# Attention and a feed-forward layer on one core: batch 1's attention divided by queries

## The chip, the core and the metric

The kernel runs on one core of a Trainium2 chip. Its engines have a queue each and run in the order of their own queue: TensorE (PE) multiplies matrices from SBUF into PSUM, VectorE (DVE) and ScalarE (ACT) work on SBUF and PSUM, GpSimd (POOL) on SBUF, and SyncE (SP) issues DMAs. An instruction waits for others by semaphores, and everything behind it in the same queue waits with it. The metric is the device time of one execution in microseconds (us), less is better.

## The reference

Eight batches of eight heads with 576 tokens of 64 channels. Each head adds two attentions: a pooled one, over means of four neighbouring tokens, and a local one, where a token sees only those less than four away. The sum, 4608 tokens of 512 channels, goes through two matrices with g = h cos(h) between them. Everything is float32.

```python
out_d = sm_attn(q_d, k_d, v_d)            # means of 4 tokens: 144 x 144 per head
out_up = np.repeat(out_d, factor, axis=2)
mask = np.abs(pos[:, None] - pos[None, :]) < factor
...
out_local = np.matmul(attn, v)
x = (out_up + out_local)                  # to 4608 x 512
h = x @ w_in                              # 512 x 2048
g = h * np.cos(h)
return g @ w_out                          # 2048 x 512
```

## The kernel before

**Tiles and steps.** The 4608 tokens are cut into 12 tiles of 384 (`TT`), and the 2048 hidden channels into 16 chunks. A step is one tile with one chunk: `gemm1` (L741, 12 matmuls: the product is made of three, of high and low parts), an elementwise chain that makes g and splits it (L752 ACT, L753 DVE, L750 and L751 ACT with Sin and Square, L756 DVE, L758 or L759 the high part `gh`, L399 the low part `gl`), and, two steps later, `gemm2` (L777, 9 matmuls into PSUM banks). `PASSES` orders the steps: the first three tiles take four chunks each in turn (steps 0 to 3 tile 0, 4 to 7 tile 1, 8 to 11 tile 2, then the next four chunks, and so on to step 47), since the weights come in by and by. From step 48 on each tile takes all 16 chunks.

**Attention.** A unit is one batch and one pair of heads (four pairs a batch): `u_qk` and `u_v` load and pool, `u_s` makes scores and softmax (on PE L546 local and L555 pooled scores; on DVE L569 adds the mask, L574 and L582 take maxima, L399 subtracts, L610 to L614 sum and invert, L616 scales; on ACT L593 to L597 the Exp), `u_t` transposes (L634 on DVE, L650 on PE, L465 copies), and `u_pv` multiplies by v (L667 pooled, L679 local), adds both (L698) and writes the high and low parts of x (L713, L399) into the tile's buffers `x0h`, `x0l` and so on. Batches 0 and 1 (`b < NEARLY`) take one form, batches 2 to 7 another (scores at L539, output at L686, over a buffer `ptb`). 576 tokens are one and a half tiles: batch 0 fills tile 0 and half of tile 1, batch 1 the other half of tile 1 (its first 192 queries) and tile 2 (the other 384), batch 2 begins tile 3.

**Weights.** Each chunk's two matrices come as 64-bit floats, are loaded to `wdi` and `wdo` (L410) and split into high and low parts `wi` and `wo` (`w_split`, L420 to L433 and L399) over a small staging buffer `xxh`. Until the last of them is split, that buffer holds the place of tile 3's x. Buffers of late chunks (`wxi`, `wxo`) hold the q, k, v and softmax of batch 0's and 1's pairs 1 to 3 until those are through.

**Order.** Nothing is looped on the chip: a planner (`Plan`) takes every operation with a time at which it is wanted (`at(time, function, batch, pair)`; the time counts steps), gives it to an engine by its own costs (some may go to one of two engines), and writes out each engine's queue. In batch 1 (L833 to L835) `u_s` of pair i is wanted at -0.9 + i, `u_t` at -0.1 + i, `u_pv` at 0.7 + i. Where the planner expects PE to idle in the first 300 us, it puts fillers (L900): products of the identity that nobody reads, which keep the clock of PE up. ACT loads a table when it goes from Exp to Sin or back.

**The mask** of batches 0 and 1 (L325 to L342) has `NSEG + 1` = 7 segments of 32 float32 columns. POOL makes all of them by `affine_select`, and two segments get an edge for the first and the last token.

Of the kernel before, what the change touches and what calls it, by code (L numbers as in the profile page):

```python
# [300 lines left out]
def attn_ffn_kernel(ctx: ExitStack, tc: tile.TileContext, qT, kT, vdn, vl, w_in, w_out, out):  # L301
# [208 lines left out]
    def u_s(b, pr):  # L510
# [57 lines left out]
        for h in range(2):  # L568
            using(banks[h], pl.op("DVE", _dve(NSEG * BS), lambda h=h: dve.tensor_tensor(  # L569
                out=sml.get()[:, NSEG * h:NSEG * (h + 1)], in0=banks[h].get()[:, LQ:LQ + NSEG * BS].rearrange("p (s n) -> p s n", n=BS),  # L570
                in1=mask[:, h:h + NSEG] if b < NEARLY else band, op=ALU.add), r=[loc[h]] + zeroed[:1], pw=[sml]))
# [16 lines left out]
        m, su2 = 4 * SD, pl.buf(None)
        bd = lambda t: t.unsqueeze(3).broadcast_to([HD, 2, 2, SD])
        if early:  # L590

            def exps():
                act.activation(mxd.get(), mxd.get(), AF.Copy, scale=1.0 / 128.0)  # L593
                act.activation(sml.get(), sml.get(), AF.Exp, scale=0.125)
# [8 lines left out]
        else:  # L603
            def exps():
                act.activation(sml.get(), sml.get(), AF.Exp, scale=0.125)
                return act.activation(smd.get(), smd.get(), AF.Exp, scale=1.0 / 128.0)
# [1 line left out]
        for sm, part, size in ((sml, sul, n), (smd, sud, m)):
            if not (early and sm is smd):
                pl.op("DVE", _dve(size), lambda sm=sm, part=part: dve.tensor_reduce(  # L610
                    out=part(), in_=sm.get(), axis=AX.X, op=ALU.add), r=[sm, su], pw=[su2])
# [3 lines left out]
        for sm, part, size, bc in ((sml, sul, n, bl), (smd, sud, m, bd)):  # L615
            f = lambda e, sm=sm, part=part, bc=bc: lambda: e.tensor_tensor(out=sm.get(), in0=sm.get(), in1=bc(part()), op=ALU.mult)  # L616
# [11 lines left out]
    def u_t(b, pr):  # L628
# [14 lines left out]
        for h in range(2):  # L643
            bk = bank(b, "t")

            def t_mm(h=h, bk=bk):
                for kh in range(2):
                    for qh in range(2):
                        o = kh * SD + qh * HD
                        pe.transpose(bk.get()[:HD, o:o + HD], smd.get()[:, h, qh, kh * HD:(kh + 1) * HD], ident[:HD, :HD])  # L650
# [325 lines left out]
```

## Time and profile before

| | us |
|---|---|
| median of 3 runs | 1002.34 (1000.7 to 1004.37) |
| the profiled execution | 1000.14 |
| its span, first to last instruction | 998.3 |
| mean granted clock of PE | 0.996 |

A row of a view by lines reads: line, engine, operation, output<-input by the program's names, shape, count; then the busy time in us and the mean of one in ns; then how long the engine idled ahead of them, and for whom. A row of a timeline begins with the start and the duration in us, and ends, in brackets, with the idle time ahead of it. A row of the table by stage gives the stage in us and its length, then the busy time of PE, PEld (weight loads), DVE, ACT and POOL, each with its count, then the clock granted to PE (1.00 is full), the share of the DMA engines in use and GB/s. A row of waits names who waited for whom, the sum in us, how often, and the longest.

### The profile page before, as it was taken

Reading aid. Unit: us, or ns where it says so; the run is one execution under the profiler, and the core shown is the slowest. Engines: PE = TensorE matmul, PEld = TensorE weight load, DVE = VectorE, ACT = ScalarE, POOL = GpSimd, SP = SyncE. Lnnn points to the kernel's source line nnn. Section 1 sums busy time; section 2 is a strip of 40 time slices with the busy share of each in tenths; the row PEclk is TensorE's granted clock in tenths of the full one; section 3 lists DMA queues with packets and bytes.
Section 4 is the critical chain, followed back from the end, with each engine's and each line's share of the span. In section 5 each row is a group of like instructions: output and inputs, shape, how many; then the busy total and the mean of one; then the engine's idle time right before and its main releaser. Section 6 shows DMA issues by size and latency. Waiting matters only on the chain.

```text
span 998.3 us, 23933 instructions
## 1 busy us (share of the span) xinstructions
PE 984.4 (99%) x9958; PEld 847.8 (85%) x9958; DVE 678.2 (68%) x1362; ACT 610.1 (61%) x1174; POOL 227.3 (23%) x280
## 2 busy tenths in 40 slices
PE   8998999999999999999999999999999999999998
PEld 5566898899888888989888888888898888899997
DVE  6899999985698677464758957565658865433433
ACT  4467687876667647555556746555646665555554
POOL 6795334621344012010002202100002200000000
PEclk9899999999999999999999999999999999999999
DMA  8876723342464222110213312201212310000000
GB/s 236 251 246 214 232 107 52 68 64 40 79 139 118 75 73 57 60 50 28 77 49 93 102 44 74 69 25 37 64 53 74 124 53 7 35 1 1 32 1 32
DMA packets 41051, 80.70 MB, mean 81 GB/s; under 512 B 4976, under 2 KB 16240, under 8 KB 40944
## 3 DMA queue, kind: packets, MB, share of 16 engines
q1 hardware_dynamic: 37056, 72.11, 23.1%
q0 software_dynamic: 3888, 7.08, 5.0%
q8 instruction: 78, 1.28, 0.5%
q14 instruction: 29, 0.24, 0.1%
HBM read 57.93 MB, written 16.52 MB: 75 GB/s over the span
## 4 chain that ended last, share of the span: by engine, by line
PE 86%; DVE 3%; DMA 1%; ACT 1%; issue 1%; POOL 1%; SPq 0%; ACTq 0%; DVEq 0%; POOLq 0%
PE bank L777 39%; PE bank L741 38%; PE bank L539 2%; PE bank L686 2%; PE bank L555 1%; PE bank L667 1%; PE bank L650 1%; DMA q<-qT 1%; SPq L641 0%; DVE su L610 0%; DVE smd L616 0%; DVE tr L756 0%; PE bank L900 0%; DMA ptb<-sml 0%; DVE tr L753 0%
## 5 line engine op out<-in xcount | busy, mean ns | idle before, releaser
L777 PE MATMUL bank<-wo,gh 128*128 128x512 f32 x1152 | 363.5, 396 | 0.0
L777 PEld LDWEIGHTS bank<-wo,gh 128*128 128x128 f32 x1152 | 210.0, 188 | 38.0 <-issue 3.3
L777 PE MATMUL bank<-wo,gl 128*128 128x512 f32 x576 | 227.6, 395 | 0.0
L752 ACT ACTIVATE tr<-bank,bmagic 128x384 f32<-128x384 f32 x192 | 110.9, 577 | 116.2 <-PE bank L741 112.3
L756 DVE SCALAR_TENSOR_TENSOR tr<-tr,bank 128x384 f32<-128x384 f32 x192 | 104.9, 546 | 107.9 <-ACT tr L751 107.1
L753 DVE SCALAR_TENSOR_TENSOR tr<-tr,bank 128x384 f32<-128x384 f32 x192 | 105.7, 550 | 82.0 <-ACT tr L752 80.3
L750 ACT ACTIVATE tr<-tr 128x384 f32<-128x384 f32 x192 | 100.7, 524 | 75.9 <-DVE tr L753 75.3
L758 ACT ACTIVATE gh<-tr 128x384 fp32r<-128x384 f32 x163 | 85.3, 523 | 88.6 <-DVE tr L756 86.9
L399 DVE TENSOR_TENSOR gl<-tr,gh 128x384 fp32r<-128x384 f32 x154 | 92.4, 600 | 63.5 <-ACT gh L758 60.6
L777 PEld LDWEIGHTS bank<-wo,gl 128*128 128x128 f32 x576 | 108.0, 188 | 23.4
L741 PE MATMUL bank<-x0h,wi 128*128 128x384 f32 x384 | 107.0, 339 | 0.0
L741 PE MATMUL bank<-x1h,wi 128*128 128x384 f32 x384 | 106.9, 339 | 0.0
L741 PE MATMUL bank<-x2h,wi 128*128 128x384 f32 x384 | 106.8, 339 | 0.0
L741 PE MATMUL bank<-x3h,wi 128*128 128x384 f32 x384 | 106.5, 338 | 0.0
L399 POOL TENSOR_TENSOR gl<-tr,gh 128x384 fp32r<-128x384 f32 x38 | 44.9, 1183 | 269.6 <-DVE gh L759 183.8
L751 ACT ACTIVATE tr<-tr 128x384 f32<-128x384 f32 x192 | 100.8, 525 | 6.1
L741 PEld LDWEIGHTS bank<-x0h,wi 128*128 128x128 f32 x384 | 70.2, 188 | 2.4 <-DVE mxl L574 0.2
L741 PEld LDWEIGHTS bank<-x1h,wi 128*128 128x128 f32 x384 | 70.2, 188 | 2.4 <-issue 0.4
L741 PEld LDWEIGHTS bank<-x2h,wi 128*128 128x128 f32 x384 | 70.2, 188 | 2.2 <-DVE xxh L425 0.2
L741 PEld LDWEIGHTS bank<-x3h,wi 128*128 128x128 f32 x384 | 70.2, 188 | 2.0
L741 PE MATMUL bank<-x3l,wi 128*128 128x384 f32 x192 | 64.6, 336 | 0.4 <-DVE x3l L399 0.4
L741 PE MATMUL bank<-x1l,wi 128*128 128x384 f32 x192 | 64.5, 336 | 0.0
(199 smaller groups left out, 1456.3 us busy)
## 6 DMA issues: line engine op xcount, KB each, us to landing
vl<-vl SPq DMA_DIRECT2D x26, 384.0 KB
out<-ob SPq DMA_DIRECT2D x36, 256.0 KB
wdi<-w_in SPq DMA_DIRECT2D x16, 512.0 KB
wdo<-w_out SPq DMA_DIRECT2D x16, 512.0 KB
q<-qT SPq DMA_DIRECT2D x26, 292.0 KB
k<-kT SPq DMA_DIRECT2D x26, 292.0 KB
vd<-vdn SPq DMA_DIRECT2D x26, 288.0 KB
out<-ob POOLq DMA_DIRECT2D x27, 256.0 KB, 5.0
```

Source lines behind the costliest of these rows:

```text
L399: f = lambda e: lambda: e.tensor_tensor(out=out(), in0=in0(), in1=in1(), op=ALU.subtract)
L539: pe.matmul(banks[h].get()[BS * g:BS * (g + 1), c:c + BS], q.get()[hs, o:o + BS], k.get()[hs, o:o + BS], start=True, stop=True)
L555: pe.matmul(banks[h].get()[:HD, i * SD:(i + 1) * SD], qkd.get()[hs, 0, i * HD:(i + 1) * HD], qkd.get()[hs, 1, :], start=True, stop=True)
L686: pe.matmul(banks[e].get()[64 * h:64 * h + 64, o:o + 2 * BQ], v4[r, NSEG * h + n, :], pt[r, :, NSEG * h + n, :BQ], start=True, stop=True)
L741: pe.matmul(ph.get()[:, :m], w[:, i, kc, :], x[:, kc, :], start=(n == 0), stop=(n == 3 * KC - 1))
L750: act.activation(tr.get(), tr.get(), AF.Sin, scale=PI)
L751: return act.activation(tr.get(), tr.get(), AF.Square)
L752: pl.op("ACT", _act(m, True, 1), lambda: act.activation(tr.get(), h(), AF.Identity, bias=bmagic), r=[ph], w=[tr])
L753: pl.op("DVE", _dve(m), lambda: dve.scalar_tensor_tensor(out=tr.get(), in0=tr.get(), scalar=MAGIC, in1=h(), op0=ALU.subtract, op1=ALU.subt ...
L756: pl.op("DVE", _dve(m), lambda: dve.scalar_tensor_tensor(out=tr.get(), in0=tr.get(), scalar=0.5, in1=h(), op0=ALU.subtract, op1=ALU.mult), ...
L758: pl.op("ACT", _act(m, False), lambda: act.activation(gh.get(), tr.get(), AF.Copy), r=[tr], w=[gh], alts=[("DVE", _dve(m / 2), lambda: dve ...
L777: pe.matmul(o, (gh, gh, gl)[k].get()[:, sl], wo.get()[:, (0, 1, 0)[k]], start=(c == c0 and k == 0), stop=(c == c1 - 1 and k == 2))
```

## The change

Batch 1's units are divided. `PART = ((0, 1), (1, 3))` counts thirds of the queries: part 0 is the first 192, part 1 the other 384. `part_s`, `part_t` and `part_pv` do for a part what `u_s`, `u_t` and `u_pv` did for the whole, with the same instructions on fewer queries: 4 or 8 of the 12 local segments, 48 or 96 of the 144 pooled queries (as partitions of one score matrix, where the whole had two of 72). Buffers are cut out of the pair's own by `piece`. All four pairs' part 0 are wanted from -0.9 on, all part 1 from 3.1 on. `smd` gets 128 partitions, so the other forms name the part of it that they use (`[:HD]`).

The mask becomes nine segments in bf16. POOL makes one, DVE copies it to the others; batch 0's second bank takes segments 3 to 8 in place of 1 to 6, and the parts take 0 to 3 and 1 to 8.

```diff
-    mask = const.tile([P, NSEG + 1, BS], F32, name="mask")
+    mask = const.tile([P, 9, BS], BF16, name="mask")
...
-        pool.memset(mask, 0.0)
+        pool.memset(mask[:, 1:2], 0.0)
         for i in range(4):
-            h = mask[i * BS:(i + 1) * BS]
+            h = mask[i * BS:(i + 1) * BS, 1:2]
...
+        dve.tensor_copy(mask[:, 0:1], mask[:, 1:2])
+        dve.tensor_copy(mask[:, 2:9], mask[:, 1:2].broadcast_to([P, 7, BS]))
...
+    PART = ((0, 1), (1, 3))
...
+    def part_s(b, pr, part):
...
+        a0, a1 = PART[part]
+        na, ns, M = a1 - a0, 4 * (a1 - a0), 48 * (a1 - a0)
...
+        def l_mm():
+            for n in range(4 * a0, 4 * a1):
+                for h in range(2):
+                    for e in range(2):
...
+        def d_mm():
+            for h in range(2):
+                hs = slice(64 * h, 64 * h + 64)
+                pe.matmul(banks[h].get()[:M, :SD], qkd.get()[hs, 0, 48 * a0:48 * a1], qkd.get()[hs, 1, :], start=True, stop=True)
...
+            in1=mask[:, a0:a0 + ns], op=ALU.add), r=[loc], w=[sml]))
...
+        def exps():
+            act.activation(mxd.get()[:M], mxd.get()[:M], AF.Copy, scale=1.0 / 128.0)
+            act.activation(sml.get(), sml.get(), AF.Exp, scale=0.125)
+            for h in range(2):
+                ins = act.activation(smd.get()[:, h], banks[h].get()[:M, :SD], AF.Exp, bias=mxd.get()[:M, h:h + 1], scale=1.0 / 128.0,
+                                     accum_out=sud()[:, h:h + 1])
...
+    def part_t(b, pr, part):
...
+    def part_pv(b, pr, part):
...
+        tt = tile_of(b * S + 192 * a0)
+        a, m = b * S + 192 * a0 - FROM[tt], 192 * na
...
+    def u_s(b, pr, part=None):
+        if part is not None:
+            return part_s(b, pr, part)
...
-                in1=mask[:, h:h + NSEG] if b < NEARLY else band, op=ALU.add), r=[loc[h]] + zeroed[:1], pw=[sml]))
+                in1=mask[:, 3 * h:3 * h + NSEG] if b < NEARLY else band, op=ALU.add), r=[loc[h]] + zeroed[:1], pw=[sml]))
...
-        for t, f in ((-4.0 + 0.5 * i, u_qk), (-2.4 + 0.5 * i, u_v), (-0.9 + i, u_s), (-0.1 + i, u_t), (0.7 + i, u_pv)):
+        for t, f in ((-4.0 + 0.5 * i, u_qk), (-2.4 + 0.5 * i, u_v)):
             at(t, f, 1, i)
+        for piece_, t0 in ((0, -0.9), (1, 3.1)):
+            for d, f in ((0.0, u_s), (0.8, u_t), (1.6, u_pv)):
+                at(t0 + i + d, f, 1, i, piece_)
```

The planner makes new queues out of this. On PE, before, the last pair of batch 1 stands directly ahead of tile 1's first GEMM (`x1h` with chunk 0's weights), between fillers (L900); L539 and L555 behind them are batch 2's first scores:

```order
L650 MATMUL bank<-ident,wxi_218 72x72 x8
...
L667 MATMUL bank<-wxo_275 64x144 x4
...
L900 MATMUL bank<-ident_b 128x512
L679 MATMUL bank<-wxi_564,wxo_587 64x24 x48
...
L539 MATMUL bank<-k,q 32x32 x48
L555 MATMUL bank<-qkd 72x144 x4
L741 MATMUL bank<-x1h,wi_947 128x384
```

Now, at the end of the same attention (L619 transposes, L649 local output and L638 pooled output of a part; L907 is `gemm1`, L943 `gemm2`, L1069 the filler):

```order
L638 MATMUL bank<-wxi_208 64x96 x4
L907 MATMUL bank<-x1h,wi_1443 128x384
...
L649 MATMUL bank<-wxo_398,wxi_551 64x24 x32
L943 MATMUL bank<-wo_1224,gh 128x512 x2
...
L619 MATMUL bank<-ident,wxi_220 72x96 x4
L649 MATMUL bank<-wxi_556,wxo_585 64x24 x32
L638 MATMUL bank<-wxo_277 64x96 x4
L1069 MATMUL bank<-ident_b 128x512
...
L701 MATMUL bank<-k,q 32x32 x48
L717 MATMUL bank<-qkd 72x144 x4
...
L907 MATMUL bank<-x2h,wi_911 128x384
```

All four GEMM steps of tile 1 have moved between the parts of the attention, and what follows the last pair is tile 2's first GEMM. In all, PE has 82 fillers ahead of step 0 and 84 from there to tile 1's first GEMM before; now 80 ahead of step 0 and 57 from there to tile 2's first GEMM.

On ACT, before, around the last pair's Exp (L594, L597 behind a table load) there stands one change of tables for the pair:

```order
L593 ACTIVATE mxd<-mxd 72x4
L594 ACT_TABLE_LOAD
L594 ACTIVATE wxi_564<-wxi_564 128x384
L597 ACTIVATE wxi_218,su<-bank,mxd 72x144 x4
...
L750 ACT_TABLE_LOAD
L750 ACTIVATE tr<-tr 128x384
```

Now each part 1 has that, between the GEMM steps of tiles 0 and 1 (here pair 2's; L916 is the Sin of a GEMM step, L959 the copy of an output):

```order
L576 ACTIVATE mxd<-mxd 96x2
L577 ACT_TABLE_LOAD
L577 ACTIVATE wxo_398<-wxo_398 128x256
L579 ACTIVATE wxo_205,su<-bank,mxd 96x144 x2
L918 ACTIVATE tr<-bank,bmagic 128x384
L959 ACTIVATE ob<-bank 128x512 x3
...
L916 ACT_TABLE_LOAD
L916 ACTIVATE tr<-tr 128x384
```

Behind the first load there are five more up to the last pair before, and nine now.

On PE ahead of step 48, the first GEMM of tile 3, batch 2's pair 3 (L667, L686; now L833, L852) stands a step earlier, before:

```order
L667 MATMUL bank<-ptd,vd 64x144 x4
L686 MATMUL bank<-ptb,vl 64x48 x24
L777 MATMUL bank<-wo_3018,gh 128x512 x2
...
L741 MATMUL bank<-x2h,wi_3202 128x384
...
L777 MATMUL bank<-wo_3116,gh 128x512 x2
...
L741 MATMUL bank<-x3h,wi_947 128x384
```

and now:

```order
L833 MATMUL bank<-ptd,vd 64x144 x4
L852 MATMUL bank<-ptb,vl 64x48 x24
L943 MATMUL bank<-wo_2990,gh 128x512 x2
...
L1069 MATMUL bank<-ident_b 128x512
...
L907 MATMUL bank<-x3h,wi_911 128x384
```

13 fillers have come in there, and three more at steps 16 and 30. Batch 2's pair 1, whose scores stood in step 19, has them in step 38. From tile 3's first GEMM on, PE's queue is the same as before.

More of the change, by code (lines that the diff above doesn't have):

```diff
@@ new lines, in part_t, with t_mm @@
+    def part_t(b, pr, part):
+        pl.name = "u_t"
+        u = st[(b, pr)]
+        a0, a1 = PART[part]
+        ns, M = 4 * (a1 - a0), 48 * (a1 - a0)
+        sml, smd = u[("sml", part)], u[("smd", part)]
+        if not part:
+            u["ptl"], u["ptd"] = ub(b, pr, "ptl"), ub(b, pr, "ptd")
+        ptl = u[("ptl", part)] = piece(u, "ptl", 4 * a0 * BS, [P, ns, BS])
+        ptd = u[("ptd", part)] = piece(u, "ptd", 192 * part, [HD, 4, M])
+        pl.op("DVE", _dve(ns * BS), lambda: dve.transpose(ptl.get().rearrange("p s q -> p (s q)"),
+                                                          sml.get().rearrange("p s n -> p (s n)")), r=[sml], w=[ptl])
+        bk = bank(b, "t")
+        def t_mm():
+            for h in range(2):
+                for kh in range(2):
+                    o = (2 * h + kh) * M
+                    pe.transpose(bk.get()[:HD, o:o + M], smd.get()[:, h, kh * HD:(kh + 1) * HD], ident[:M, :M])
+        pl.op("PE", 4 * 0.0009 * M + 0.05, t_mm, r=[smd], w=[bk], util=0.4)
+        evac(4 * M, ptd.get, lambda: bk.get()[:HD, :4 * M].rearrange("p (a n) -> p a n", a=4), bk, ptd)
@@ L605, in exps @@
                 act.activation(sml.get(), sml.get(), AF.Exp, scale=0.125)
[L606 removed]
+                return act.activation(smd.get()[:HD], smd.get()[:HD], AF.Exp, scale=1.0 / 128.0)
             pl.op("ACT", _act(n, False) + _act(m, False), exps, w=[sml, smd], tab="exp")
[L608 removed]
+        for sm, part, size, np_ in ((sml, sul, n, P), (smd, sud, m, HD)):
             if not (early and sm is smd):
[L610 to L611 removed]
+                pl.op("DVE", _dve(size), lambda sm=sm, part=part, np_=np_: dve.tensor_reduce(
+                    out=part(), in_=sm.get()[:np_], axis=AX.X, op=ALU.add), r=[sm, su], pw=[su2])
         pl.op("DVE", 0.1, lambda: dve.tensor_scalar(out=su.get(), in0=su.get(), scalar1=1e-9, scalar2=2.0 * PI,
@@ L614, in u_s @@
         pl.op("DVE", 0.15, lambda: dve.reciprocal(su.get(), su.get()), w=[su])
-        for sm, part, size, bc in ((sml, sul, n, bl), (smd, sud, m, bd)):
-            f = lambda e, sm=sm, part=part, bc=bc: lambda: e.tensor_tensor(out=sm.get(), in0=sm.get(), in1=bc(part()), op=ALU.mult)
+        for sm, part, size, bc, np_ in ((sml, sul, n, bl, P), (smd, sud, m, bd, HD)):
+            f = lambda e, sm=sm, part=part, bc=bc, np_=np_: lambda: e.tensor_tensor(out=sm.get()[:np_], in0=sm.get()[:np_], in1=bc(part()), op=ALU.mult)
             alts = [("DVE", _dve(size), f(dve))]
@@ L626, in u_s, with u_t @@
         u["sml"], u["smd"] = sml, smd
-    def u_t(b, pr):
+    def u_t(b, pr, part=None):
+        if part is not None:
+            return part_t(b, pr, part)
         pl.name = "u_t"
@@ L654, in u_t, with u_pv @@
         u["ptl"], u["ptd"] = ptl, ptd
-    def u_pv(b, pr):
+    def u_pv(b, pr, part=None):
+        if part is not None:
+            return part_pv(b, pr, part)
         pl.name = "u_pv"
```

119 lines of the change are left out of this document (110 added, 9 removed).

## The prediction

> **What bounds the kernel now.** I read the page first: its busy shares, and the chain that ended last.
>
> ```profile
> PE 984.4 (99%) x9958; PEld 847.8 (85%) x9958; DVE 678.2 (68%) x1362; ACT 610.1 (61%) x1174; POOL 227.3 (23%) x280
> PE 86%; DVE 3%; DMA 1%; ACT 1%; issue 1%; POOL 1%; SPq 0%; ACTq 0%; DVEq 0%; POOLq 0%
> ```
>
> TensorE is busy for 99% of the span, but part of that is filler: L900 multiplies the identity by itself so that the clock stays up. The view of that line and the timeline of PE show where filler ends.
>
> ```profile
> L900 PE MATMUL bank<-ident_b x166: 376/379/634, 1.4 to 102.7; 128*128 128x512 bf16 x166
> 49.68 0.52 PE L741 MATMUL bank<-x0h,wi 128*128 128x384 f32 x1
> 99.08 1.25 PE L900 MATMUL bank<-ident_b 128*128 128x512 bf16 x5
> 100.26 1.59 PE L679 MATMUL bank<-wxi,wxo 32*64 32x24 f32 x96
> 104.57 0.44 PE L741 MATMUL bank<-x1h,wi 128*128 128x384 f32 x1
> 305.33 0.33 PE L741 MATMUL bank<-x3h,wi 128*128 128x384 f32 x1
> ```
>
> Five fillers take 100.26 - 99.08 = 1.18 us, so 0.236 us each. All 166 stand before 102.7 us. The first GEMM (step 0) starts at 49.68, the first GEMM of tile 1 (step 4) at 104.57, the first of tile 3 (step 48) at 305.33. What PE waits for behind 104.5 us, to the end of the span, is all of this:
>
> ```profile
> PE bank L650 <- DVE smd L616: 0.8, 1, 0.8
> PE bank L741 <- DVE x3l L399: 0.4, 1, 0.4
> PE bank L686 <- DMA ptb<-sml: 0.2, 1, 0.2
> ```
>
> So from 104.57 on the kernel is a queue of matmuls with 1.4 us of waits. The time is set by when that dense part begins and by how much is left then. Ahead of it, the table by stage shows who is full.
>
> ```profile
> 50.00:62.50 12.50, 12.28 (x167) 7.38 (x166) 12.06 (x26) 5.39 (x19) 11.88 (x13) 1.00 0.90 286
> 62.50:75.00 12.50, 11.90 (x253) 8.66 (x251) 11.91 (x24) 10.48 (x26) 12.11 (x13) 1.00 0.59 204
> 75.00:87.50 12.50, 11.26 (x247) 7.97 (x246) 11.46 (x20) 10.06 (x25) 8.80 (x10) 1.00 0.33 89
> 87.50:100.00 12.50, 10.98 (x149) 6.94 (x147) 12.14 (x30) 9.23 (x23) 5.59 (x5) 1.00 0.96 339
> ```
>
> The third busy figure is DVE: 47.6 of 50 us (95%). PE, with its fillers, is idle for 3.6 us there. The attention of batch 1 runs on a full VectorE, while PE has four GEMM steps of tile 0 to do and fills up with L900.
>
> **The change, part by part.** Tile 1 needs only the first 192 queries of batch 1. With them done first, the four GEMM steps of tile 1 go under the attention of the other 384, and the dense part begins at step 8 in place of 4. From the chain of waits, one step is 2.10 + 2.08 = 4.18 us:
>
> ```profile
> 201.19 2.10 PE bank L741 x12
> 203.29 2.08 PE bank L777 x9
> ```
>
> Four steps are **16.7 us** less behind the dense start. What matters is how much later that start (T, the first GEMM of tile 2) comes than 104.57. PE's own sum between step 0 and T takes the attention pieces from the timeline, start to start:
>
> ```profile
> 57.77 0.67 PE L650 MATMUL bank<-ident,smd 72*72 72x72 f32 x8
> 58.27 0.38 PE L900 MATMUL bank<-ident_b 128*128 128x512 bf16 x1
> 58.58 1.05 PE L546 MATMUL bank<-xxl 64*32 64x32 f32 x96
> 59.56 0.71 PE L555 MATMUL bank<-wxi 64*72 64x144 f32 x8
> 60.20 0.71 PE L667 MATMUL bank<-ptd,vd 72*64 72x144 f32 x8
> 60.85 2.76 PE L900 MATMUL bank<-ident_b 128*128 128x512 bf16 x12
> 65.64 1.59 PE L679 MATMUL bank<-sml,vl 32*64 32x24 f32 x96
> 67.16 1.68 PE L900 MATMUL bank<-ident_b 128*128 128x512 bf16 x7
> ```
>
> Local scores (L546) take 0.98, pooled scores (L555) 0.64, transposes (L650) 0.50, pooled output (L667) 0.65, local output (L679) 1.52 us. Both parts together multiply the same columns, so I price them alike.
>
> - Before, step 0 to step 4: 84 fillers 19.8, four first GEMMs 8.4, two second GEMMs 4.2, four pairs' transposes and outputs 10.7, three pairs' scores 4.9, scores of batch 2's first pair 1.6: 49.6 us. It took 104.57 - 49.68 = 54.9, so 5.3 us were lost to waits.
> - After, step 0 to step 8: 57 fillers 13.5, eight first GEMMs 16.8, six second 12.5, attention 10.7 + 6.2 + 1.6 (a third of pair 0's local scores stands ahead of step 0): 61.3 us.
>
> Step 0 itself has less ahead of it on PE (two fillers, and two thirds of pair 0's local and all of its pooled scores: 1.8 us), but its operands come from DVE: I put it at 49.0. For the waits I take 4 us, a little under the 5.3 of before, since PE is planned without filler in the second half. **T = 49.0 + 61.3 + 4 = 114.3.**
>
> DVE checks this. Its work on batch 1 lies between its first and its last row there: 105 instructions in 103.0 - 49.1 = 53.9 us, at 95% some 51 of work. The new order has 167 from the first row to the last.
>
> ```profile
> 49.09 0.62 DVE L569 TENSOR_TENSOR sml<-bank,mask 128x192 f32<-128x192 f32 x2 [0.24 <-PE bank L555]
> 102.21 0.82 DVE L698 TENSOR_TENSOR wxi<-bank,wxi 128x288 f32<-128x288 f32 x2 [0.78 <-ACT wxi L465]
> ```
>
> ```profile
> L427 DVE SCALAR_TENSOR_TENSOR xxh<-wdo,xxh 128x512 int32<-128x512 int32 x4 | 3.7, 931 | 0.0
> L582 DVE TENSOR_REDUCE mxd<-bank 72x2 f32<-72x288 f32 x8 | 3.5, 443 | 0.0
> L753 DVE SCALAR_TENSOR_TENSOR tr<-tr,bank 128x384 f32<-128x384 f32 x4 | 2.2, 540 | 0.0
> L574 DVE TENSOR_REDUCE mxl<-wxi 128x12 f32<-128x384 f32 x2 | 1.1, 538 | 0.0
> ```
>
> 288 and 384 elements (L582, L574) differ by 95 ns, about 1 ns an element, so 0.16 us of an instruction doesn't shrink with its size; some 36 more halves are 5.8 us at most, and 3 where neighbours overlap. Ten more GEMM instructions (4 of L753, 3 of L756, 3 casts), none above 0.54, are 5; seven more of weight splitting, none above L427's 0.93, are 5; three pooled sums of 576 elements taken from POOL, at 0.73 by that slope, 2. Subtractions and products given to POOL (2,300 elements) take 2.3 off, and up to 5 with the waits they had. I take 10 more: 61 us, which at 95% is 64. From 49 that ends at 113, and about 2 us of cast and x2l behind it give 115: T again, within a us.
>
> ScalarE gets four more table loads: the two parts alternate Exp and Sin nine times where the whole did five.
>
> ```profile
> 74.37 1.28 ACT L594 ACT_TABLE_LOAD   x1
> 75.66 0.53 ACT L594 ACTIVATE wxo<-wxo 128x384 f32<-128x384 f32 x1
> ...
> 78.93 0.52 ACT L750 ACTIVATE tr<-tr 128x384 f32<-128x384 f32 x1
> 79.92 0.27 ACT L465 ACTIVATE wxi<-bank 128x144 f32<-128x144 f32 x1
> ```
>
> The load at 74.37 costs 1.28 us and the Exp behind it starts 0.01 us later; four are 5.1 us. Sin and Square (78.93 to 79.92) take 0.99. From the first Sin load to the last x2h the order gives ACT about 38 us (nine loads 11.5, eight pairs of Sin and Square 7.9, the rest at its durations in the trace), beside 39 us of PE: covered, with little to spare. [...]
>
> Behind T, the order shows 16 fillers where before had none: 13 ahead of step 48, 3 earlier. They are real matmuls: 16 x 0.236 = **3.8 us**. The planner sets them where it expects PE to wait, and x3l is just in time already (the 0.4 us above). From the first GEMM of tile 3 on, PE's order is the old one.
>
> Small edits: the mask is built on 32 columns in place of 224 and copied by two DVE instructions; they stand ahead of pooled sums whose first reader, L555, starts at 8.04 us, and DVE idles till 8.86, which hides about 1 us. A bf16 operand beside an f32 one from PSUM is in no row; between half of L569's 0.31 us and twice it, eight such instructions of batch 1 move DVE by -1.2 to +2.5 us. I take none, as the PSUM operand stays. Loads stand in the old order through the fourth weight chunk.
>
> **Sum**: 104.57 + 16.7 - 114.3 - 3.8 = 3.2 us gained. The profiled execution took 1000.14 us with a span of 998.3 and 1.84 around it; it would become 996.9. It lies 2.2 below the median of the runs (1002.34), to which I apply the same gain: **999.1 us**.
>
> **Rivals.** *The clock stays up.* In before it fell to half while batch 0 ended:
>
> ```profile
> 40.00:42.00 2.00, 1.34 (x37) 1.29 (x39) 0.00 (x0) 0.00 (x0) 1.84 (x4) 0.69 0.99 329
> 42.00:44.00 2.00, 2.00 (x11) 1.01 (x10) 0.59 (x2) 0.29 (x1) 1.84 (x5) 0.50 0.92 285
> 43.41 0.46 DVE L698 TENSOR_TENSOR wxi<-bank,wxi 128x288 f32<-128x288 f32 x1 [3.68 <-ACT wxi L465]
> ```
>
> DVE lost 3.68 us to it. There the new order has 32 local scores in place of 96 and more fillers, so the dip may not come. For it: the narrow matmuls that preceded it are moved. Against: the same outputs of the last two pairs remain. Step 0 would come at 45.3; with 2 us of waits T = 108.6, and the gain is 8.9: 993.4. [...]
>
> *Three full engines wait for each other.* PE 39, ACT 38 and DVE 35 us in the second half leave no slack for in-order queues. With twice the waits (10 us, and step 0 at 49.7) T = 121.0 and the change loses 3.5: 1005.8; midway nothing changes, about 1002.5.
>
> *Batch 2 is late for tile 3, and it is slower.* The order has moved batch 2's pair 1 from steps 19 to 23 to step 38 on, right ahead of pairs 2 and 3.
>
> ```profile
> 278.53 0.97 PE bank L539 x66
> 262.00:305.00 43.00, 43.00 (x653) 36.68 (x652) 35.82 (x76) 28.63 (x51) 18.40 (x24) 1.00 0.55 131
> ```
>
> Pair 3 had its scores at 278.53 and gave x3l 29 us later, with DVE at 83%. If the third pair in a row makes x3l come 6.3 us after PE would be ready, the fillers' 3.1 us and the whole gain are gone; beyond that it is slower, and at 10 us by 3.7: about 1006. Against it: pairs 2, 3 and the next stood equally close before.
>
> *Each switch of tables holds ACT for longer than its load.* If it were another load's time (1.28 us by the row at 74.37), nine would add 11.5 us, ACT would have 49.5 us to do where PE has 39, and T would be near 124: slower by 6.5, 1008.8. The rows at 74.37 and 75.66 speak against it. [...]
>
> **How the numbers follow.** Forecast (gain 1 to 5.5) 0.46; clock stays up 0.22; engines wait 0.20; batch 2 late 0.10; longer switches 0.02. 0.3% (3 us) is about what a measurement of this kernel tells from no change. The forecast lies on that edge: 0.28 of it beyond, 0.18 within. Faster 0.28 + 0.22 = 0.50; same 0.18 + 0.14 + 0.02 = 0.34; slower 0.06 + 0.08 + 0.02 = 0.16. The range goes from the clock's case to the first loss, 993 to 1005.5.
>
> **What would show it.** PE's first GEMM of tile 2 near 114 us; four GEMM steps of tile 1 between 75 and 110; nine table loads of 1.28 us with the next ACTIVATE at once; DVE still above 90% to 110; 13 fillers and little wait ahead of tile 3's first GEMM, near 302. Wrong if T is past 121, if PE idles over 3 us ahead of tile 3 beside the fillers, or if steps 8 to 16 wait for split weights.

## The result, and the profile after

The divided kernel takes 1009.5 us (median; 1007.31 to 1014.58) beside 1002.34 for the kernel before on the same chip: a ratio of 1.0064, with an interval of 1.0034 to 1.0093. It is **slower** by about 6 us where a gain of 3.2 was forecast. One more execution of it, at 1192.44 us with a granted clock of 0.75, and the profiled one of e5 further down, at 1577.66 us with 0.56, fell into a slow state of the chip and are left out of these figures. The profiled execution took 1007.31 with a span of 1005.0, 6.7 more than the span before.

The page's busy shares and its chain of waits:

```profile
PE 987.8 (98%) x9977; PEld 845.7 (84%) x9977; DVE 687.3 (68%) x1418; ACT 615.7 (61%) x1180; POOL 213.9 (21%) x272
PE 86%; DVE 6%; POOL 3%; issue 2%; DMA 2%; ACT 1%; SPq 0%; ACTq 0%; POOLq 0%; DVEq 0%
```

The page doesn't say where the time went: PE is as full as it was, and its chain has some more DVE, POOL and issue in it. The timeline of PE does, at the four places that the prediction speaks of: step 0, tile 1 (step 4), tile 2 (step 8, T) and tile 3 (step 48). The last row is tile 2 in the kernel before.

```profile
44.40 0.53 PE L907 MATMUL bank<-x0h,wi 128*128 128x384 f32 x1
...
85.90 0.44 PE L907 MATMUL bank<-x1h,wi 128*128 128x384 f32 x1
...
119.44 0.69 PE L907 MATMUL bank<-x2h,wi 128*128 128x384 f32 x1
...
312.62 0.44 PE L907 MATMUL bank<-x3h,wi 128*128 128x384 f32 x1
...
121.42 0.33 PE L741 MATMUL bank<-x2h,wi 128*128 128x384 f32 x1
```

In the kernel before tile 2 began at 121.42 and tile 3 at 305.33. So T came 2.0 us earlier (7 were forecast), and the way from T to step 48 took 193.2 us in place of 183.9 (3.8 more were forecast). From step 48 on the order is the old one: the spans differ by 6.7, the starts of step 48 by 7.3. Both losses lie ahead of 313 us, in two places.

**The first place: step 0 to T.** The table by stage, cut at steps 0, 2, 7 and 8, then the stage around T:

```profile
44.40:73.40 29.00, 26.10 (x392) 14.03 (x390) 26.13 (x73) 16.10 (x48) 18.84 (x28) 1.00 0.75 221
73.40:105.50 32.10, 31.96 (x516) 25.80 (x513) 31.32 (x75) 27.02 (x57) 22.90 (x26) 1.00 0.31 97
105.50:119.40 13.90, 11.54 (x276) 8.55 (x272) 13.90 (x28) 11.08 (x25) 7.39 (x7) 1.00 1.01 361
```

These are three stages with different limits. In the first (part 0, steps 0 and 1) no engine is full: PE, with 50 fillers in it, and DVE have 26.1 of 29.0. In the second (steps 2 to 6) PE is full, 31.96 of 32.10, and DVE nearly so (31.32). In the third DVE is full, and PE waits. The timelines of PE, DVE and POOL show the end of it:

```profile
112.58 0.55 PE L638 MATMUL bank<-wxo 72*64 72x96 f32 x8
...
115.36 0.86 PE L701 MATMUL bank<-k,q 64*32 64x32 f32 x76 [0.28 <-DVE wxi L655]
118.09 0.33 PE L701 MATMUL bank<-k,q 64*32 64x32 f32 x16 [1.87 <-issue]
```

```profile
112.40 1.49 DVE L427 SCALAR_TENSOR_TENSOR xxh<-wdi,xxh 128x512 int32<-128x512 int32 x1
113.82 1.22 DVE L423 TENSOR_SCALAR xxh<-xxh 128x512 f32<-128x512 f32 x1
114.96 0.61 DVE L655 TENSOR_TENSOR wxi<-bank,wxi 128x192 f32<-128x192 f32 x2
```

```profile
112.00 1.35 POOL L401 TENSOR_TENSOR x2l<-wxo,x2h 128x384 fp32r<-128x384 f32 x1 [1.20 <-ACT x2h L666]
113.31 1.45 POOL L401 TENSOR_TENSOR gl<-tr,gh 128x384 fp32r<-128x384 f32 x1
116.20 1.28 POOL L401 TENSOR_TENSOR x2l<-wxi,x2h 128x384 fp32r<-128x384 f32 x1 [1.45 <-ACT x2h L666]
```

PE has multiplied the last pair at 113.1, and needs its x2l. The sum of that pair (L655) stands in DVE's queue behind two weight splits which take 1.49 and 1.22 us with POOL's two subtractions beside them (L427 and L423 take 0.68 and 0.41 with POOL quiet, at 119.70 and 119.37). The low part itself goes to POOL, 1.28 us where DVE takes 0.55 for a low part of the same shape (gl at 117.96). So x2l is ready at 117.5. By then PE is at the scores of batch 2's first pair (L701), which stop for 1.87 us in the middle with nothing in the profile to wait for, and T is 119.44. Behind that the clock is low:

```profile
115.00:117.00 2.00, 0.94 (x80) 0.75 (x76) 2.00 (x6) 1.32 (x3) 0.80 (x1) 1.00 1.05 376
117.00:119.00 2.00, 0.91 (x25) 0.68 (x25) 2.00 (x3) 0.98 (x2) 0.49 (x1) 1.00 1.05 373
119.00:121.00 2.00, 1.94 (x8) 1.65 (x7) 1.72 (x5) 0.68 (x1) 0.00 (x0) 0.59 0.30 110
121.00:123.00 2.00, 2.00 (x9) 2.00 (x8) 0.00 (x0) 0.00 (x0) 0.00 (x0) 0.56 0.02 8
```

**The second place: ahead of step 48.** PE's timeline behind the last pair's output (L852, 304.67), DVE's beside it, and POOL's x3l:

```profile
307.69 0.39 PE L943 MATMUL bank<-wo,gl 128*128 128x512 f32 x1
307.92 0.61 PE L1069 MATMUL bank<-ident_b 128*128 128x512 bf16 x2
309.49 1.25 PE L1069 MATMUL bank<-ident_b 128*128 128x512 bf16 x5 [0.96 <-DVE vd L864]
310.97 1.59 PE L1069 MATMUL bank<-ident_b 128*128 128x512 bf16 x6 [0.23 <-DVE vd L864]
```

```profile
306.32 0.75 DVE L492 TENSOR_REDUCE qkd<-q 128x144 f32<-128x576 f32 x1 [1.71 <-DMA q<-qT]
306.99 0.68 DVE L506 TENSOR_TENSOR vd<-vd 72x512 f32<-72x512 f32 x1
...
308.99 0.44 DVE L864 TENSOR_TENSOR vd<-bank,xd 128x288 f32<-128x288 f32 x1
...
310.47 0.44 DVE L864 TENSOR_TENSOR vd<-bank,xd 128x288 f32<-128x288 f32 x1
```

```profile
311.56 0.99 POOL L401 TENSOR_TENSOR x3l<-vd,x3h 128x384 fp32r<-128x384 f32 x1 [11.95 <-ACT x3h L879]
```

From 307.92 to 312.62, 4.7 us, PE has nothing but 13 fillers (3.5 us) and 1.2 us of labelled waits. DVE is not full there; its queue waits 1.71 us for the q of a later batch and does that batch's pooling ahead of the sums (L864) on which tile 3 depends. Its x3l is through on POOL at 312.55. Step 47 to step 48 took 4.2 us before and 10.8 now.

### The profile page after: what moved, and what is told of

It reads as the page before. It is cut to its first block, busy times and chain, and to the rows that moved or that the text cites. A ratio compares the mean times of both kernels' runs of the same rounds, so it can differ in the third digit from the quotient of the medians.

```text
span 1005.0 us, 24020 instructions
## 1 busy us (share of the span) xinstructions
PE 987.8 (98%) x9977; PEld 845.7 (84%) x9977; DVE 687.3 (68%) x1418; ACT 615.7 (61%) x1180; POOL 213.9 (21%) x272
## 3 DMA queue, kind: packets, MB, share of 16 engines
q8 instruction: 78, 1.28, 0.5%
## 4 chain that ended last, share of the span: by engine, by line
PE 86%; DVE 6%; POOL 3%; issue 2%; DMA 2%; ACT 1%; SPq 0%; ACTq 0%; POOLq 0%; DVEq 0%
PE bank L943 37%; PE bank L907 37%; PE bank L701 2%; PE bank L852 2%; PE bank L717 2%; PE bank L833 2%; PE bank L814 1%; PE bank L1069 1%; DMA q<-qT 1%; DVE xxh L429 1%; DVE gl L401 0%; DVE xxh L423 0%; POOL wxi L487 0%; DVE xxh L425 0%; DVE xxh L427 0%
## 5 line engine op out<-in xcount | busy, mean ns | idle before, releaser
L943 PE MATMUL bank<-wo,gh 128*128 128x512 f32 x1152 | 364.4, 397 | 0.0
L943 PEld LDWEIGHTS bank<-wo,gh 128*128 128x128 f32 x1152 | 209.5, 188 | 38.7 <-issue 4.0
L943 PE MATMUL bank<-wo,gl 128*128 128x512 f32 x576 | 227.7, 396 | 0.6 <-DVE gl L401 0.6
L918 ACT ACTIVATE tr<-bank,bmagic 128x384 f32<-128x384 f32 x192 | 110.7, 577 | 113.8 <-PE bank L907 108.7
L916 ACT ACTIVATE tr<-tr 128x384 f32<-128x384 f32 x192 | 100.6, 524 | 81.4 <-DVE tr L919 80.9
L924 ACT ACTIVATE gh<-tr 128x384 fp32r<-128x384 f32 x164 | 85.9, 524 | 90.0 <-DVE tr L922 88.3
L943 PEld LDWEIGHTS bank<-wo,gl 128*128 128x128 f32 x576 | 108.0, 187 | 24.5 <-DVE gl L401 1.0
L907 PE MATMUL bank<-x0h,wi 128*128 128x384 f32 x384 | 107.3, 340 | 1.2 <-POOL wi L401 1.1
L907 PE MATMUL bank<-x2h,wi 128*128 128x384 f32 x384 | 108.0, 342 | 0.1
L907 PE MATMUL bank<-x1h,wi 128*128 128x384 f32 x384 | 107.7, 341 | 0.4 <-DVE tr L922 0.3
L907 PE MATMUL bank<-x3h,wi 128*128 128x384 f32 x384 | 106.6, 338 | 0.1
L907 PEld LDWEIGHTS bank<-x0h,wi 128*128 128x128 f32 x384 | 70.1, 188 | 4.0 <-POOL wi L401 1.4
L907 PEld LDWEIGHTS bank<-x1h,wi 128*128 128x128 f32 x384 | 70.2, 188 | 3.7 <-DVE tr L922 1.8
L907 PEld LDWEIGHTS bank<-x2h,wi 128*128 128x128 f32 x384 | 71.2, 190 | 2.4 <-PE bank L1069 0.4
L907 PEld LDWEIGHTS bank<-x3h,wi 128*128 128x128 f32 x384 | 70.2, 188 | 2.5 <-PE bank L1069 0.6
L907 PE MATMUL bank<-x2l,wi 128*128 128x384 f32 x192 | 65.0, 339 | 0.0
L907 PE MATMUL bank<-x0l,wi 128*128 128x384 f32 x192 | 64.6, 336 | 0.1
```

The source lines that it names most:

```text
L907: pe.matmul(ph.get()[:, :m], w[:, i, kc, :], x[:, kc, :], start=(n == 0), stop=(n == 3 * KC - 1))
L916: act.activation(tr.get(), tr.get(), AF.Sin, scale=PI)
L918: pl.op("ACT", _act(m, True, 1), lambda: act.activation(tr.get(), h(), AF.Identity, bias=bmagic), r=[ph], w=[tr])
L924: pl.op("ACT", _act(m, False), lambda: act.activation(gh.get(), tr.get(), AF.Copy), r=[tr], w=[gh], alts=[("DVE", _dve(m / 2), lambda: dve ...
L943: pe.matmul(o, (gh, gh, gl)[k].get()[:, sl], wo.get()[:, (0, 1, 0)[k]], start=(c == c0 and k == 0), stop=(c == c1 - 1 and k == 2))
```

## The experiments

Starts of a step's first GEMM in us, from the timelines of PE, with the span of the profiled execution and the median of the runs (those with one run have its time). Steps 2, 7 and 8 cut the three stages; 9 and 49 lie behind the scores ahead of step 8 and behind what step 48 waits for. Each row is a single execution, and 1 to 3 us of it can be a low clock somewhere on the way (an estimate from 1.6 us behind T in the divided kernel and 3.1 between steps 0 and 2 of e6).

| kernel | 0 | 2 | 7 | 8 | 9 | 47 | 48 | 49 | span | us |
|---|---|---|---|---|---|---|---|---|---|---|
| before | 49.7 | 73.6 | 117.2 | 121.4 | 125.6 | 301.1 | 305.3 | 313.9 | 998.3 | 1002.3 |
| divided | 44.4 | 73.4 | 105.5 | 119.4 | 125.2 | 301.8 | 312.6 | 319.4 | 1005.0 | 1009.5 |
| e1 | 45.1 | 75.0 | 106.9 | 121.5 | 127.8 | 304.6 | 313.4 | 322.9 | 1009.3 | 1011.7 |
| e2 | 49.2 | 77.4 | 120.5 | 124.7 | 128.9 | 304.3 | 308.5 | 316.9 | 1001.3 | 1002.6 |
| e3 | 46.0 | 74.4 | 106.5 | 120.6 | 126.1 | 302.6 | 313.7 | 320.4 | 1006.3 | 1008.0 |
| e4 | 47.5 | 77.3 | 117.1 | 121.4 | 125.6 | 305.1 | 309.6 | 315.9 | 1003.5 | 1004.6 |
| e6 | 43.9 | 76.1 | 108.1 | 119.8 | 124.1 | 302.8 | 313.5 | 320.3 | 1004.8 | 1007.0 |
| e7 | 44.7 | 72.7 | 105.8 | 113.8 | 118.1 | 297.6 | 302.0 | 308.4 | 993.5 | 997.9 |
| e8 | 43.8 | 74.6 | 107.1 | 121.3 | 125.6 | 302.3 | 313.9 | 320.7 | 1006.2 | 1008.0 |
| e9 | 43.9 | 73.4 | 106.8 | 118.6 | 122.9 | 299.2 | 310.6 | 317.4 | 1001.8 | 1004.2 |
| e10 | 53.0 | 79.7 | 121.3 | 127.4 | 131.6 | 306.5 | 312.9 | 317.2 | 1002.2 | 1002.9 |
| e11 | 42.9 | 73.2 | 106.9 | 116.2 | 122.4 | 298.4 | 303.0 | 309.1 | 993.8 | 995.9 |
| e12 | 48.1 | 76.2 | 108.3 | 122.9 | 127.7 | 309.5 | 314.2 | 320.2 | 1007.7 | 1009.8 |
| e13 | 44.4 | 75.7 | 107.3 | 121.3 | 126.6 | 303.1 | 314.5 | 321.3 | 1009.3 | 1008.6 |
| e14 | 43.2 | 75.3 | 108.9 | 118.6 | 122.9 | 299.9 | 304.5 | 310.6 | 995.3 | 997.3 |

The kernel before was run beside each group and had medians of 1002.6 (e1 to e4), 1002.9 (e5 to e8), 1003.6 (e9 to e12) and 1003.3 (e13, e14).

**e1: 15 of the 16 fillers behind 150 us taken out.** The order is the divided kernel's. One filler, ahead of step 16, stays (at 157.1 us).

```diff
-           fgap=0.4, f0=0.8, fend=300.0, ...
+           fgap=0.4, f0=0.8, fend=200.0, ...
```

> Undivided order, only the 16 fillers behind 150 us are gone (1 ahead of step 16, 2 ahead of step 30, 13 ahead of step 48). Theory A (fillers cost their own time): 16 x 0.236 = 3.8 us less than the divided kernel, about 1005.7 by its median of 1009.5, and step 47 to 48 takes about 7.5 us in place of 10.4. Theory B (x of tile 3 is late, the fillers stand in a wait that is there anyway): at most 1 us less, and PE's wait ahead of step 48 grows from 1.2 to about 4.5 us, for DVE's or POOL's x3l.

1011.71 us, ratio 1.0077 (1.0049 to 1.0105): no gain. PE's timeline at that place:

```profile
308.88 0.91 PE L852 MATMUL bank<-ptb,vl 64*64 64x48 f32 x46 [1.14 <-DMA ptb<-sml]
309.71 0.85 PE L943 MATMUL bank<-wo,gh 128*128 128x512 f32 x2
...
313.36 0.45 PE L907 MATMUL bank<-x3h,wi 128*128 128x384 f32 x1
...
316.17 0.45 PE L907 MATMUL bank<-x3l,wi 128*128 128x384 f32 x1 [0.64 <-POOL x3l L401]
```

The GEMM of tile 3 now follows the second GEMMs at once, and then waits inside for x3l until 316.17, 6.5 us behind the last pair's output (309.7); in the divided kernel it was 6.9 (305.7 to 312.62). Steps 47 to 49 take 18.3 us, and 17.6 with the fillers. That is theory B: x3l is late, and the fillers stand in its wait. (Part of these 18.3 us is the clock, granted at 0.79 from 309 to 311 us and at 0.50 from 311 to 313: three matmuls of a second GEMM that take 0.69 us at 306.53 in the divided kernel take 1.27 at 310.80. It doesn't touch the 6.5 us, which are ACT's, DVE's and POOL's way to x3l.)

**e2: the mask alone, on the kernel before; e3: the divided kernel with a float32 mask.**

```diff
 e2, on the kernel before
-    mask = const.tile([P, NSEG + 1, BS], F32, name="mask")
+    mask = const.tile([P, 9, BS], BF16, name="mask")
...
 e3, on the divided kernel
-    mask = const.tile([P, 9, BS], BF16, name="mask")
+    mask = const.tile([P, 9, BS], F32, name="mask")
```

> The kernel before with the mask of nine bf16 segments and nothing else. Theory A (the mask does nothing): within 0.2% of the kernel before, step 0 at 49 to 50 us with the clock at 0.5 for some us ahead of it. Theory B (the mask made step 0 earlier, as in the changed kernel, 44.4): step 0 at about 45, and the dense part begins up to 4 us earlier, total 998 to 1000.

> The changed kernel with its nine segments in float32, so nearly the division alone. If the mask's type does nothing: 1009.5 within 0.2%, the same steps within 0.5 us, and the pause of 1.9 us in the scores of batch 2's first pair (L701) and the clock below 0.9 at 112 to 125 us come again. If bf16 costs DVE time: the part 0 stage (44 to 73 us) up to 1 us shorter.

e2: 1002.57 us, ratio 0.999 (0.9973 to 1.0006). e3: 1008.03, ratio 1.0047 (1.0026 to 1.0067), and in its profile the pause (1.8 us) and the low clock (0.86 at 112.5 to 125) are there again. The mask costs and brings nothing that can be measured; the loss is the division's, and what happens around T repeats.

**e4, e5, e12, e7: batch 2's attention pulled ahead.** e4 gives all units of batch 2 a boost of 10 in the plan, e5 only the attention of its pairs 1 to 3 one of 20, e7 the same three pairs one of 10. e12 is e5 once more, for its profile.

```diff
 e4
-BOOST = {0: 100.0}
+BOOST = {0: 100.0, 2: 10.0}
 e5 and e12 with 20.0, e7 with 10.0
+        if f in (u_s, u_t, u_pv) and a[0] == 2 and a[1] > 0:
+            pl.boost = 20.0
         f(*a)
```

> The changed kernel with batch 2's units pulled ahead in the plan (a boost of 10 as batch 0 has one of 100). Its first pair's scores stand behind step 11, its second pair's in step 15, its last pair's output in step 44 in place of 47, and there are no fillers ahead of step 48. Theory B (batch 2 comes late for tile 3, and its first scores hold up tile 2): 5.7 us less at step 48 (13 fillers 4.55 with gaps, waits 1.2) and 2 to 3 less at step 8, less what part 0 loses by the other order (up to 6): 1000 to 1005. Theory A (the loss lies in tile 1's and 2's attention alone, and batch 2 is no matter): 3 us less by the fillers at most, 1006 to 1010.

> The order of the changed kernel up to step 14; behind it the attention of batch 2's pairs 1 to 3 stands 1 to 6 steps earlier (last pair's output in step 44 in place of 47), with 11 fillers ahead of step 48 less (1 or 2 remain) and 9 more further ahead. If the lateness of batch 2 costs what I read (fillers 4.55 and waits 1.2 behind step 47): step 47 to 48 in 4.2 to 5 us in place of 10.8, total 4 to 6 us less than the changed kernel, 1003.5 to 1005.5; steps 0 to 8 and T (119.4) unchanged within 1 us. If PE only waits elsewhere for the same work (DVE or ACT full between 230 and 310): less than 2 us.

> The same kernel as the one with batch 2's pairs 1 to 3 pulled by 20, once more for its profile. Steps 0 to 8 as in the changed kernel (T 119 to 120.5), step 47 to 48 in 4.2 to 5 us in place of 10.8, and step 48 at 306 to 309 in place of 312.6, so that what is left over the kernel before (305.3) is T's and the scores'.

> The attention of batch 2's pairs 1 to 3 pulled ahead by 10: in this order its first pair's scores stand in step 17 and its last pair's output in step 44, and no filler stands ahead of step 48; parts 0 and 1 of batch 1 are ordered a little differently too. If both losses add: 4 to 6 us by batch 2 and 2 to 3 by the scores, 1001 to 1004. If tile 1's and 2's attention alone sets it: 1006 to 1010.

e4: 1004.59 us, ratio 1.0011 (0.9987 to 1.0035). e5: 1005.92, ratio 1.003 (1.0012 to 1.0048). e7: **997.88, ratio 0.9953 (0.993 to 0.9975)**, faster than both kernels and than the 1001 to 1004 that were expected of it. Steps 9 to 49, the way on which batch 2 is done, take 188.3 us in the kernel before, 194.2 divided, 192.5 in e12, and 190.3 in e4 and e7, which have the first pair's scores (1.6 us) in it besides. What e4 wins there it loses ahead of T: its steps 2 to 7 take 39.9 us in place of 32.1.

e12 missed: its step 47 to 48 is 4.7 us as expected, but only 1.7 us are saved from 9 to 49, and its one execution was 3.9 us slower than e5's median. Idle time and fillers of PE on that way are 6.6 us in the divided kernel, still 5.5 in e12 (11 fillers ahead of steps 16, 28 and 44, and idle time, 1.3 us of it at 261 us), 1.6 in e7 and 1.2 in the kernel before. In e12 pair 1 begins in step 35, in e7 in step 20 and pair 2 in step 26; the kernel before had pair 1 in step 19. So the place of the last pair alone doesn't win the time back. That three pairs in a row between steps 35 and 47 are what costs is read off these orders, not tested by itself. What e7 does at tile 3:

```profile
301.10 0.62 PE L943 MATMUL bank<-wo,gh 128*128 128x512 f32 x2
301.56 0.40 PE L943 MATMUL bank<-wo,gl 128*128 128x512 f32 x1
301.80 0.41 PE L814 MATMUL bank<-ident,smd 72*72 72x72 f32 x4
302.02 0.42 PE L907 MATMUL bank<-x3h,wi 128*128 128x384 f32 x1
```

No filler, no wait: step 47 to 48 in 4.4 us. And its end of batch 1:

```profile
110.13 0.55 PE L638 MATMUL bank<-wxo 72*64 72x96 f32 x8
110.61 0.73 PE L943 MATMUL bank<-wo,gh 128*128 128x512 f32 x2
...
113.50 0.61 PE L1071 MATMUL bank<-ident_b 128*128 128x512 bf16 x2 [0.40 <-ACT x2h L666]
113.75 0.53 PE L907 MATMUL bank<-x2h,wi 128*128 128x384 f32 x1
```

Up to step 7 it is as late as the divided kernel (105.8 and 105.5). Then T comes at 113.75, 5.7 us earlier: the last output ends 2.5 us sooner, 3.1 us lie behind it in place of 6.3, half of them under a second GEMM, and no scores are in the way. The plan has also put 47 fillers between step 0 and T in place of 57.

**e6: the scores of batch 2's first pair moved behind step 8.** In the divided kernel they are multiplied at 115 us and first read at 203.17, by DVE's L731.

```diff
     order = pl.schedule()
+    late = next(o for o in order if o.eng == "PE" and o.name == "u_s" and o.arg == (2, 0))
+    steps_ = [o for o in order if o.name == "gemm1" and o.eng == "PE"]
+    order.remove(late)
+    late.start = steps_[13].end
+    order.insert(order.index(steps_[13]) + 1, late)
```

> The changed kernel with one operation moved on PE: the scores of batch 2's first pair (96 + 8 matmuls) from ahead of step 8 to behind the first GEMM of step 13. If they hold up tile 2: the first GEMM of step 8 at about 117.5 (x2l's end on POOL) in place of 119.4, the clock stays above 0.95 at 112 to 125, and step 16 comes 1 to 3 us earlier than 155.0 with the 1.6 us of scores in it. If the pause is the weights' DMA's doing and hits whatever is there: step 8 at 119 again, with a pause of over 1 us elsewhere between 113 and 121.

1006.98 us, ratio 1.0038 (1.0022 to 1.0054). Steps 7 to 9 take 16.0 us in place of 19.7; 1.6 of these 3.7 are the scores themselves, which come later. No pause, no low clock behind T:

```profile
112.50:125.00 12.50, 11.79 (x122) 8.27 (x121) 12.50 (x24) 8.99 (x19) 4.80 (x5) 1.00 0.80 286
```

T itself is no earlier (119.8), as this execution lost 3.1 us between steps 0 and 2, where another low clock lies (0.73 at 50 to 62.5 us), and the plan put 13 fillers in place of 7 between step 7 and T.

**e8 and e13: work on VectorE doubled and taken away; e9: work on PE doubled.** All three have the divided kernel's order.

```diff
 e8, in part_s (the maximum likewise)
-        using(banks[0], pl.op("DVE", _dve(n), lambda: dve.tensor_tensor(
+        using(banks[0], pl.op("DVE", _dve(n), lambda: [dve.tensor_tensor(
...
-            in1=mask[:, a0:a0 + ns], op=ALU.add), r=[loc], w=[sml]))
+            in1=mask[:, a0:a0 + ns], op=ALU.add) for _ in range(2)][-1], r=[loc], w=[sml]))
...
 e13, in part_s (the subtraction and the sum likewise)
-        ... dve.tensor_reduce(out=mxl.get()[:, :ns], in_=sml.get(), axis=AX.X, op=ALU.max) ...
+        ... dve.tensor_reduce(out=mxl.get()[:, :1], in_=sml.get()[:, :1], axis=AX.X, op=ALU.max) ...
 e9, in part_s (the transposes of part_t likewise)
-                pe.matmul(banks[h].get()[:M, :SD], qkd.get()[hs, 0, 48 * a0:48 * a1], ...)
+                for _ in range(2):
+                    pe.matmul(banks[h].get()[:M, :SD], qkd.get()[hs, 0, 48 * a0:48 * a1], ...)
```

> In each part the add of the mask and the maximum of the local scores are issued twice on VectorE (16 instructions more, 0.20 to 0.36 us each, 4.9 us in all; the result is the same). If VectorE is what sets the start of tile 2: T 4 to 5 us later (123.5 to 124.5), half of it by step 2 to 4. If PE's own pieces set it, VectorE's work goes into its idle time: T within 1.5 us of 119.4.

> The changed kernel with the maximum, the subtraction and the sum of the local scores of batch 1's parts done for one segment of 32 columns in place of all 4 or 8 (the softmax of the others is left without them; the same instructions in the same order). About 4 us less work between step 0 and T, 3 to 3.5 of it on VectorE. If VectorE's work sets T, as half of what was added came through when it was doubled: step 0 to T 1.5 to 3.5 us shorter (75.1), total 1 to 3 us below the changed kernel. If T hangs on latencies from engine to engine: less than 1 us.

> The changed kernel with each part's pooled scores and transposes issued twice on PE (per pair 0.38 + 0.41 and 0.30 + 0.41 us more, 6.0 in all for four pairs; the result is the same). If PE's own pieces set the way from step 0 to T: T 5 to 6 us later relative to step 0 (81 in place of 75.1 us). If PE has slack there (it idles 5.0 us and has 56 fillers of 15.2 us in the way): at most 3 us later, most of it between steps 3 and 8, where PE is busy for 49.9 of 50.5 us.

e8: 1008.0 (one run). e13: 1008.64, ratio 1.0042 (1.0019 to 1.0065). e9: 1004.22 (one run), less than the kernel that has 6 us less to do. The second stage, steps 2 to 7, in the three (first e8, then e13, then e9):

```profile
74.60:107.10 32.50, 31.79 (x514) 25.68 (x513) 32.22 (x82) 25.88 (x57) 21.93 (x26) 1.00 0.29 90
```

```profile
75.70:107.30 31.60, 31.60 (x514) 25.80 (x513) 29.51 (x75) 26.23 (x55) 21.41 (x26) 1.00 0.33 99
```

```profile
73.40:106.80 33.40, 33.40 (x540) 27.53 (x537) 31.03 (x76) 26.82 (x56) 23.29 (x27) 1.00 0.30 92
```

With DVE 1.8 us lighter than in the divided kernel the stage is 0.5 shorter, and PE fills it to the last; with 1.8 us more on PE (L557 0.77, L621 1.0) it is 1.3 longer. So PE sets this stage, with DVE close behind it (0.9 us more on DVE in e8 make it 0.4 longer). The first stage isn't set by PE: e9's 1.8 us more there make it 0.5 longer. What DVE does to it can't be told, as steps 0 to 2 take 30.8 (e8) and 31.2 us (e13) with a clock of 0.94 and 0.89 there. Steps 7 to 8 take 14.2 and 14.0 in e8 and e13 and 11.8 in e9, with DVE full in all three. In e9 the scores run without a pause, and the clock stays up (1.00 over 112.5 to 125 us):

```profile
116.24 1.36 PE L703 MATMUL bank<-k,q 64*32 64x32 f32 x96
...
118.62 0.45 PE L909 MATMUL bank<-x2h,wi 128*128 128x384 f32 x1
```

From step 0 to T the three take 77.5 (e8), 76.9 (e13) and 74.7 us (e9) beside 75.0. For VectorE 4 to 5 us more were expected in e8 and 1.5 to 3.5 less in e13, for PE 5 to 6 more in e9. Neither engine's work by itself sets T.

**e10: the pull of e7 on the kernel before, undivided.**

> The kernel before, undivided, with the same pull of 10 on the attention of batch 2's pairs 1 to 3. If that pull is worth something by itself: 3 us or more less than the kernel before, so that the gain of the divided kernel with it is not the division's. If it only mends what the division's order broke: 1001.5 to 1005, the kernel before within 0.2%.

1002.92 us, ratio 0.998 (0.9961 to 0.9998): at the edge of what can be told, and less than half of e7's gain by the medians. The two intervals still touch (e7's ends at 0.9975); that of e11, below, ends at 0.9952. So what e7 wins is hardly the pull's alone.

**e11: a pull of 12, and the scores moved behind step 8; e14: the pull of 12 alone.**

> The divided kernel with a pull of 12 in place of 10 and the scores of batch 2's first pair moved on PE from ahead of step 8 to behind its first GEMM. If the early start of tile 2 (113 to 115 us) and an unhurried step 48 are what the gain of the run with 10 consists of: the same gain here, 996 to 1000, T 113 to 116, step 48 at 301 to 304. If the order with 10 was a lucky one: 1001 to 1006.

> As the divided kernel with a pull of 12, but with the scores of batch 2's first pair left ahead of step 8. Against the run with them moved (995.9): if the scores cost what they did in the changed kernel (a pause of up to 1.9 us, and the clock behind it), 1.5 to 3 us more, 997.5 to 999, and the pause is there again in PE's waits. If the pause needs the other order: within 1 us.

e11: **995.9 us, ratio 0.9923 (0.9894 to 0.9952)**. e14: 997.27, ratio 0.9947 (0.9913 to 0.9981). The order of e7 was not a single lucky one: two more gain as much, and T and step 48 of e11 (116.2 and 303.0) are within 0.2 us of what was expected. The two differ by 1.4 us, less than their intervals; in e14 the scores stand ahead of T and run in 0.95 us, without a pause. So the place of the scores costs little by itself; the pause does, and it needs more than that place.

## Why the prediction was wrong, step by step

**What bounds the kernel**: right from step 48 on, where the order and the time are the old ones. From T to step 48 it was a queue of matmuls before, and no longer is: 2.2 us of idle time and 4.4 of fillers lie there now.

**"Four steps are 16.7 us less behind the dense start"**: right. Tile 1's first GEMMs stand at 85.9 to 107.9, between 75 and 110 as forecast, under the attention of part 1.

**"T = 49.0 + 61.3 + 4 = 114.3"**: this step failed; T is 119.44. Step 0 came 4.6 us earlier than I put it, at 44.4: the rival of the clock that stays up came true there (the granted clock is 1.00 at 37.5 to 50 us). It isn't all: e12, with the same order up to there and the same clock, has step 0 at 48.1. From step 0 to T took 75.0 us in place of 65.3. At the prediction's own prices the three stages of PE's sum are 21.9, 29.2 and 10.2 us; they took 29.0, 32.1 and 13.9. So the term that failed is that of the waits: 4 us, where 13.7 were lost:

- 7.1 in the first stage. Idle time of PE is 2.9 of it, fillers at 0.26 in place of 0.236 us 1.2, the GEMMs 1.1, and the shorter attention pieces about 2 (they don't shrink as their queries do: a matmul of the pooled output takes 0.046 us with 48 columns, and 0.080 with 144 in the kernel before). No engine is full there; that four short units in turn hang on the way from engine to engine is argued, not shown by a run.
- 2.9 in the second. Here PE is the limit (e9, e13), and a GEMM with attention pieces on both sides takes 2.3 us, not the 2.10 and 2.08 of the dense part: ten of them, 2.4 us.
- 3.7 in the third. The pause of 1.87 us is half of it; e9, which has none, takes 11.8 us there. DVE is full, with slow splits, and x2l is on POOL.

The check on DVE gave 115, and x2l was through at 117.5: DVE did 66.4 us of work from its first row on batch 1 to its last, not 61, but started 3.5 us earlier, and "about 2 us of cast and x2l behind it" were 1.9. So the agreement of the two within a us was no support for either. The scores of batch 2's first pair, 1.6 us in the sum, took 4.2 with their pause and pushed T to 119.4.

**"Late fillers, 3.8 us"**: wrong in kind. From T to step 48 9.3 us were lost: 4.4 of fillers as they stand in the timeline, 2.2 of idle time, 2.0 and 0.5 on first and second GEMMs (1.6 of it the low clock behind T), 0.2 on the rest. And the fillers were no cost of their own (e1). They stand in a wait for x3l, which is the rival *batch 2 is late for tile 3*, given 0.10: pair 1 stood in step 38, right ahead of pairs 2 and 3, and x3l came 4.7 us after PE was ready. I had priced it to decide from 6.3 us on, but against a T of 114.3, and had read the fillers as the plan's caution when they were the plan's own forecast of that wait.

**ACT, "covered, with little to spare"**: right. Nine table loads of 1.28 us, and what follows each starts within 0.02 us, as in

```profile
99.41 1.28 ACT L916 ACT_TABLE_LOAD   x1
100.70 0.53 ACT L916 ACTIVATE tr<-tr 128x384 f32<-128x384 f32 x1
```

**The mask**: rightly taken at nothing (e2, e3).

**The size that was forecast** is there once both places are mended: e7 has T at 113.8 and tile 3 without a wait, and takes 997.88 us by its median, where 999.1 was forecast with T at 114.3. That T agrees is luck in part: step 0 came 4.3 us earlier than I put it, and the way from there took 69.1 us in place of 65.3, with ten fillers less in it than the sum had. With a better order the division is worth its place; the order that came with it lost more than that.

What no run tested: why the scores pause in the order of the divided kernel (e1, e3, e12 and e13 have it too, at 1.5 to 1.8 us, e8 at 1.1) and not in e9 or e14. The stretch has the DMA engines at 1.05 of their share (376 GB/s over 115 to 117 us) in the divided kernel and at 1.02 (366 GB/s) in e9 over steps 7 to 8, so that alone is not it. In all six executions the pause stands behind the same matmul, 80 of the 96. In the divided kernel it lasts from 116.2 to 118.1, and a piece of DMA queue q8, one of 78 of 16384 bytes, takes from 115.5 to 116.6: the page's row, then the same over 115.5 to 116.7 us.

```profile
q8 instruction: 78, 1.28, 0.5%
q8 instruction: 1, 0.02, 5.6%
```

Whether the pause is a wait for that piece no run shows.

## What to carry to other kernels

A sum of one engine's own pieces bounds a stage only where that engine is full in the changed order; where several short units follow one another, cut the stage at its limits and give the hand-overs from engine to engine a term of their own (here 7 us of 29 in one stage, where 4 of 65 had been allowed for all). Fillers that appear in a planned order are a message: the plan expects a wait there, so ask what for before pricing them as work. And when a change moves a deadline early, look at what the planner puts off in exchange: here three pairs of batch 2, which cost more than the early start brought.
